# Gated delta attention and a GELU MLP on one core: the first chunk's inverse blocks go through DRAM on one queue, in the program's order

## The chip, the core and the metric

The kernel runs on one core of a Trainium2 chip. The core has five instruction streams that the profile names PE (TensorE, the matrix engine), DVE (VectorE), ACT (ScalarE), POOL (GpSimd) and SP (SyncE, which here only issues DMAs). DMAs are issued by SP, ACT and POOL. The metric is the device time of one execution in microseconds (us); lower is better.

## What is computed

Two blocks follow each other. The first is a delta-rule attention over 4 batches, 8 heads, 768 tokens and a head width of 48. The second is an MLP on the 3072 tokens with 384 inputs, 2048 hidden units and a sigmoid-approximated GELU. Cut to what matters:

```
k_n = k / (norm(k) + 1e-6)
for t in range(S):                      # per batch and head, state is 48 x 48
    y[t]  = q[t] @ state                # read before the update
    v_old = k_n[t] @ state
    state = state + beta[t] * outer(k_n[t], v[t] - v_old)
x = y, heads side by side               # 3072 x 384
h = x @ w_in                            # 384 x 2048, given as float64
out = (h / (1 + exp(-1.702 * h))) @ w_out   # 2048 x 384, given as float64
```

## The kernel before

**Chunks and units.** The 768 tokens are cut into 6 chunks of 128. A unit is one chunk of one batch (all 8 heads), so there are 24 units; units 0 to 3 are chunk 0, units 4 to 7 chunk 1. Within a chunk the recurrence is solved as a triangular system. The 128 tokens of a unit are four blocks of 32. For each head and block the inverse of a 32 x 32 triangular matrix is needed (tile `XB`, one per unit), and the rest is matmuls.

**What a unit needs.** `prepare(n)` transposes keys and queries on PE into `psT`, ACT copies them to `kqT` (L324), PE forms key-key and query-key products `psG` (L337), and ACT or DVE copies those into the SBUF tile `G` (L341, L343, L345). Then SP writes part of `G` to DRAM (`Nd`, L349) and reads its diagonal blocks back into `NT` with another layout (L355), and POOL masks the other half of `G` (L361).

**The inverse.** `invert(c, b0, nb)` takes the diagonal blocks in `NT`, one (batch, head, block) per partition, and inverts them on DVE by substitution: 15 steps of a multiply and a reduce (L401, L405 or, with the order kept, L104), then two rounds of four (L384, L385). For chunk 0 it runs once for all four batches on 128 partitions; for later chunks it runs for two batches at a time, mixed into the other work. Its result is scaled into `YS` (L435, tag `P`, which has two buffers that are also used by the temporaries of the weight conversion). `YS` has the wrong layout for PE, so each batch's quarter is written to DRAM (`Yd`, L439) and read back as `XB` (L444). In chunk 0, before the change, batches 0 and 2 use the SP queue and batches 1 and 3 the ACT queue. Each `XB` read waits for its `Yd` write.

**Solving.** Class `Step` holds a unit's chain: `solve` multiplies the inverse of a block with the values (`psU`, L490), `solved` copies to `U` on ACT (L497), `above` multiplies what has been solved into the next block (`psR`, L478), `rest` subtracts it from the values on DVE (`V`, L486). Four such rounds make a unit; `state` (L522, L530) and `outputs` (`psY`, L503; copies L542, L543; small DMAs L549 into `xT`) follow. `slot(n, share)` runs three units at different blocks side by side and puts pieces of the MLP between them.

**The MLP.** `hidden` multiplies `xT` with `w_in` (`ph`, L565) and applies the activation on ACT (`gT`, L570); `written` multiplies with `w_out` (`po`, L580), copies on DVE (L587) and stores. The weights come as float64 and are turned into float32 by bit operations in `from_double`: on DVE L167, then L173, L174, L175, L176, and for all but the first three pieces one step on ACT (L172) between L167 and L175. There are 12 pieces of `w_in` (the first three convert on DVE alone, pieces 4 to 12 with L172; they are called conversions 1 to 9 below) and 16 of `w_out`. POOL fetches most of the raw pieces (L239, L247) into space that earlier conversions have freed.

**Fillers.** `warm(n)` issues n matmuls on constants that only keep PE busy (`ps_warm`, L138): 80 at the start, 48 at the end of chunk 0's substitution, 6 in each of many groups of the first slots.

**Order.** The framework plans the order of instructions on each engine from its own estimates; the order in the program is only a starting point. An operation that goes through `pinned` (shown in profiles with line L104) keeps its place in the program's order. Each engine then works its list from front to back.

Of the kernel before, what the change touches and what calls it, by code (L numbers as in the profile page):

```python
# [18 lines left out]
def kernel(  # L19
# [19 lines left out]
    nc = tc.nc  # L39

    B, H, S, D = q.shape
# [60 lines left out]
    def pinned(op):  # L102

        return lambda *a, **kw: tc.keep_in_program_order(op(*a, **kw))  # L104
# [9 lines left out]
    for blk in range(NB):  # L114
# [10 lines left out]
        out=YB, in_=YB, compare_op=ALU.not_equal, fill=1.0, base=0,  # L125
# [6 lines left out]
    def warm(n, after=None):  # L132

        ps = ps_moe.tile([128, 256], F32, tag="moe", name="ps_warm")
        if after is not None:
            after(ps[:, 0:1], 0.0)
        for _ in range(n):
            nc.tensor.matmul(ps, lhsT=ones[:, 0:128], rhs=ones, start=True, stop=True)  # L138
# [229 lines left out]
    def invert(c, b0=0, nb=B):  # L368

        np = nb * NB * H  # L370
        part = slice(b0 * NB * H, b0 * NB * H + np)
        N, Y = NT[part], YB[part]
        bc = bI[part, c].broadcast_to([np, BS, BS])
        tt, red = nc.vector.tensor_tensor, nc.vector.tensor_reduce
        if c == 0:
            tt, red = pinned(tt), pinned(red)
        tt(N, N, bc, op=ALU.mult)  # L377
        yield 0.0
        HS = BS // 2

        def dots(o, a, b, ny, nx, nk, negate):

            P = wk.tile([128, ny, nx, nk], F32, tag="P", name="P")[part]
            tt(P, a, b, op=ALU.mult)  # L384
            red(o, P, axis=AX.X, op=ALU.add, negate=negate)  # L385

        def halves(t):

            return [t[:, s * HS : (s + 1) * HS, s * HS : (s + 1) * HS] for s in range(2)]


        Yf = Y.rearrange("p j i -> p (j i)")
        Nf = N.rearrange("p i k -> p (i k)")
        step = HS * BS + HS

        def diag(t, off, dims):
            return bass.AP(t.tensor, t.offset + off, [t.ap[0], [step, 2]] + dims)

        for i in range(1, HS):
            P = wk.tile([128, 2, i, i], F32, tag="P", name="P")[part]  # L400
            tt(  # L401
                P, diag(Nf, i * BS, [[0, i], [1, i]]), diag(Yf, 0, [[BS, i], [1, i]]),
                op=ALU.mult,
            )
            red(diag(Yf, i, [[BS, i]]), P, axis=AX.X, op=ALU.add, negate=True)  # L405
            yield 0.0


        X1 = N[:, 0:HS, HS:]
        nc.scalar.activation(X1, halves(Y)[1].rearrange("p l i -> p i l"), ACT.Copy)  # L410
        A = N[:, 0:HS, 0:HS]
        N10, Y0 = N[:, HS:, 0:HS], halves(Y)[0]
        Q = 4
        for j in range(0, HS, Q):
            n = HS - j
            dots(
                A[:, j : j + Q, :],
                N10[:, :, j:].rearrange("p (o l) k -> p o l k", o=1).broadcast_to([np, Q, HS, n]),
                Y0[:, j : j + Q, j:].rearrange("p j (o k) -> p j o k", o=1).broadcast_to([np, Q, HS, n]),
                Q, HS, n, False,  # L420
            )
            yield 0.0
        for i in range(0, HS, Q):
            n = i + Q
            dots(
                Y[:, 0:HS, HS + i : HS + i + Q],
                A[:, :, 0:n].rearrange("p j (o l) -> p j o l", o=1).broadcast_to([np, HS, Q, n]),
                X1[:, i : i + Q, 0:n].rearrange("p (o i) l -> p o i l", o=1).broadcast_to([np, HS, Q, n]),
                HS, Q, n, True,
            )  # L430
            yield 0.0
        if c == 0:
            warm(NY, pinned(nc.vector.memset))
        YS = wk.tile([128, BS, BS], F32, tag="P", name="YS")[part]
        nc.vector.tensor_tensor(YS, Y, bc, op=ALU.mult)  # L435
        for b in range(b0, b0 + nb):
            Yd = dram.tile([H * C, BS], F32, tag="Yd", name="Yd", bufs=4)
            eng = nc.scalar if c == 0 and b % 2 == 1 else nc.sync
            eng.dma_start(  # L439
                out=Yd.rearrange("(p j) i -> p j i", j=BS),  # L440
                in_=YS[(b - b0) * NB * H : (b - b0 + 1) * NB * H],
            )
            XB = wk.tile([128, H, BS], F32, tag="XB", name="XB", bufs=4)
            eng.dma_start(out=XB, in_=Yd.rearrange("(h t) i -> t h i", h=H))  # L444
            inverse[c * B + b] = XB
        yield 0.0


    def bank(name, shape=(128, H, D)):
        return ps_seq.tile(list(shape), F32, tag="seq", name=name)  # L450
# [3 lines left out]
    class Step:  # L454


        def __init__(self, n, xT):
            self.c, self.b = units[n]
            self.xT = xT
            self.kn, self.kqT, self.G = ready.pop(n)  # L460
            self.V, self.XB = loaded.pop(n), inverse.pop(n)
            self.psR = bank("psR")
# [25 lines left out]
        def solve(self, blk, h, psU):  # L488
            r = slice(blk * BS, (blk + 1) * BS)
            nc.tensor.matmul(  # L490
                psU[r, h, :], lhsT=self.XB[r, h, :], rhs=self.V[r, h, :],
                start=True, stop=True,
# [136 lines left out]
    def slot(n, share):  # L629
# [12 lines left out]
        for group in range(GR):  # L642
# [48 lines left out]
            if group == GR - 1 and n % HB == 1:  # L691

                m = n + 1 + HB
                if B <= m < len(units):
                    inverting = invert(*units[m], HB)
# [52 lines left out]
    for i in range(B, len(KN)):  # L748
        load(i, ((KN, k), (QP, q)), sync)
    ahead(2, sync)  # L750
    run(invert(0))
    normalize_first(B, len(KN) - B)
    run(weights(W1))
# [34 lines left out]
```

## Time and profile before

| what | value |
|---|---|
| median of 3 runs | 866.31 us (864.33 to 867.01) |
| profiled execution, its own time | 865.54 us |
| span of the profile | 863.8 us |
| PE busy | 813.2 us, 94% |
| PE weight loads busy | 601.8 us, 70% |
| DVE busy | 489.7 us, 57% |
| ACT busy | 208.6 us, 24% |
| POOL busy | 104.8 us, 12% |
| mean granted PE clock | 0.96 |

The span is the part of the execution that the profiler's records cover. All times in views of the profile count from its start. A line of a timeline gives the start, the length, the engine, the line of the kernel, the operation, the tiles as out<-in, the count, and in brackets how long the engine had been idle and what ended that.

### The profile page before, as it was taken

To read this page: it belongs to the slowest core of one execution; us is meant where nothing else is said; L and a number is where in the kernel's file an instruction comes from. 1 tells how busy PE (TensorE), PEld (TensorE's weight loads), DVE (VectorE), ACT (ScalarE), POOL (GpSimd) and SP (SyncE) were. 2 spreads that over 40 slices of the span, in tenths; PEclk is the share of its full clock that TensorE was granted. 3 is DMA by queue.
4 is the path that set the end of the run, shared out by engine and by line. 5 is a ranking of instruction groups with operands and counts; after the bars stand their busy time and mean duration, and the time that the engine had idled before them with its cause. 6 is when DMAs were issued, how large, how long until landed. Compare 5 with 4: busy or idle time off the path is not lost.

```text
span 863.8 us, 15545 instructions
## 1 busy us (share of the span) xinstructions
PE 813.2 (94%) x6564; PEld 601.8 (70%) x6564; DVE 489.7 (57%) x1024; ACT 208.6 (24%) x407; POOL 104.8 (12%) x117
## 2 busy tenths in 40 slices
PE   8309899989999999999999999999999999999998
PEld 7207688757767867867867767767767768677684
DVE  5898569979983592682682772772872851110100
ACT  3202345333212312312312312213212102112020
POOL 2103131230022102102102101101100000000000
PEclk9759759999999999999999999999999999999999
DMA  9995653451422223122132132132032020000000
GB/s 145 181 153 118 152 153 77 111 141 33 83 59 56 52 48 82 36 68 63 35 71 66 29 83 57 25 85 51 12 77 51 2 57 2 10 14 1 18 6 18
DMA packets 160964, 55.75 MB, mean 65 GB/s; under 512 B 128672, under 2 KB 157568, under 8 KB 160896
## 3 DMA queue, kind: packets, MB, share of 16 engines
q1 hardware_dynamic: 151872, 45.50, 26.0%
q0 software_dynamic: 1856, 7.87, 2.9%
q10 hardware_dynamic: 7168, 1.41, 1.3%
q8 instruction: 51, 0.84, 0.4%
q14 instruction: 17, 0.14, 0.1%
HBM read 33.13 MB, written 20.45 MB: 62 GB/s over the span
## 4 chain that ended last, share of the span: by engine, by line
PE 87%; DVE 7%; DMA 3%; issue 1%; ACT 1%; POOL 1%; ACTq 0%; DVEq 0%; POOLq 0%
PE ph L565 30%; PE po L580 28%; PE psG L337 6%; PE psR L478 5%; PE psY L503 5%; PE psU L490 4%; PE psR L467 2%; PE psT L323 2%; PE psS L522 2%; PE ps_warm L138 2%; DVE P L104 1%; DMA QP<-in_q_dram 1%; DVE YB L104 1%; DMA w_out<-in_moe_w_out_dram 1%; DVE tmp L104 1%
## 5 line engine op out<-in xcount | busy, mean ns | idle before, releaser
L565 PE MATMUL ph<-xT,w_in 128*128 128x256 f32 (+1 forms) x1248 | 270.1, 370 | 0.1
L580 PE MATMUL po<-w_out,gT 128*128 128x384 f32 x768 | 267.3, 493 | 2.2 <-DVE w_out L176 2.2
L565 PEld LDWEIGHTS ph<-xT,w_in 128*128 128x128 f32 x1248 | 219.8, 192 | 37.5 <-issue 9.6
L580 PEld LDWEIGHTS po<-w_out,gT 128*128 128x128 f32 x768 | 139.9, 190 | 92.4 <-issue 9.2
L486 DVE TENSOR_TENSOR V<-V,psR 32x384 f32<-32x384 f32 x92 | 50.6, 550 | 97.5 <-PE psR L478 91.7
L570 ACT ACTIVATE gT<-ph 128x512 f32<-128x512 f32 (+1 forms) x104 | 58.7, 564 | 186.9 <-PE ph L565 186.8
L497 ACT COPY U<-psU 32x384 f32<-32x384 f32 x96 | 45.1, 470 | 148.3 <-PE psU L490 99.5
L478 PEld LDWEIGHTS psR<-U,G 32*32 32x32 f32 (+2 forms) x1152 | 56.7, 112 | 23.7 <-issue 21.3
L138 PE MATMUL ps_warm<-ident 128*128 128x256 bf16 x260 | 35.8, 299 | 36.1 <-DVE ps_warm L104 33.0
L478 PE MATMUL psR<-U,G 32*32 32x48 f32 (+2 forms) x1152 | 67.3, 212 | 0.5 <-ACT U L497 0.5
L337 PE MATMUL psG<-kqT 48*128 48x256 f32 x384 | 62.2, 420 | 3.9 <-ACT kqT L324 2.8
L138 PEld LDWEIGHTS <-ident 128*128 128x128 bf16 x260 | 27.4, 107 | 43.1 <-DVE ps_warm L104 34.0
L490 PEld LDWEIGHTS psU<-V,XB 32*32 32x32 f32 x1536 | 39.6, 109 | 25.2 <-issue 12.2
L361 POOL TENSOR_SCALAR_AFFINE_SELECT G<-G 128x1024 f32<-128x1024 f32 x24 | 27.0, 1124 | 248.6 <-DVE G L345 112.1
L401 DVE TENSOR_TENSOR P<-NT,YB 64x2 f32<-64x2 f32 (+4 forms) x150 | 52.3, 349 | 4.6
L587 DVE COPY o<-po 128x384 f32<-128x384 f32 x24 | 13.3, 555 | 71.9 <-PE po L580 71.7
L405 DVE TENSOR_REDUCE YB<-P 64x2 f32<-64x2 f32 (+4 forms) x150 | 48.0, 320 | 4.4
L490 PE MATMUL psU<-V,XB 32*32 32x48 f32 x1536 | 47.6, 208 | 1.3 <-DVE V L486 1.3
L341 ACT ACTIVATE G<-psG 128x512 f32<-128x512 f32 x48 | 28.7, 597 | 76.4 <-PE psG L337 76.3
L337 PEld LDWEIGHTS psG<-kqT 48*128 48x128 f32 x384 | 37.4, 194 | 13.2 <-ACT kqT L324 4.0
L542 DVE COPY last<-psY 48x128 f32<-48x128 f32 x20 | 5.9, 294 | 59.1 <-ACT xT L543 58.2
L377 DVE TENSOR_TENSOR NT<-NT,bI 64x1024 f32<-64x1024 f32 x10 | 12.2, 1219 | 45.0 <-DMA NT<-Nd 44.9
(81 smaller groups left out, 713.7 us busy)
## 6 DMA issues: line engine op xcount, KB each, us to landing
Nd<-G SPq DMA_DIRECT2D x24, 512.0 KB, 3.2
w_out<-in_moe_w_out_dram POOLq DMA_DIRECT2D x14, 384.0 KB, 4.0
KN<-in_k_dram SPq DMA_DIRECT2D x24, 192.0 KB, 3.2
V<-in_v_dram SPq DMA_DIRECT2D x24, 192.0 KB, 3.3
out_dram<-o SPq DMA_DIRECT2D x24, 192.0 KB, 1.9
QP<-in_q_dram SPq DMA_DIRECT2D x20, 192.0 KB, 3.5
w_out<-in_moe_w_in_dram SPq DMA_DIRECT2D x6, 576.0 KB, 12.1
NT<-Nd SPq DMA_DIRECT2D x24, 128.0 KB, 2.5
```

The lines of the kernel that those rows point to most:

```text
L138: nc.tensor.matmul(ps, lhsT=ones[:, 0:128], rhs=ones, start=True, stop=True)
L337: nc.tensor.matmul(ps[hh][:, i], lhsT=kqT[pr, g + i, 0, :], rhs=kqT[pr, g + i, :, :], start=True, stop=True,)
L401: tt(P, diag(Nf, i * BS, [[0, i], [1, i]]), diag(Yf, 0, [[BS, i], [1, i]]), op=ALU.mult,)
L405: red(diag(Yf, i, [[BS, i]]), P, axis=AX.X, op=ALU.add, negate=True)
L478: nc.tensor.matmul(self.psR[r, h, :], lhsT=self.G[a, h, 0, r], rhs=self.U[a, h, :], start=(self.c == 0 and h == 0), stop=True, skip_group_ ...
L486: nc.vector.tensor_tensor(self.V[r], self.V[r], self.psR[r], op=ALU.subtract)
L490: nc.tensor.matmul(psU[r, h, :], lhsT=self.XB[r, h, :], rhs=self.V[r, h, :], start=True, stop=True,)
L497: nc.scalar.copy(self.U[r], psU[r])
L503: nc.tensor.matmul(self.psY[p : p + D, j, :], lhsT=lhsT(h), rhs=rhs(h), start=start and j == 0, stop=True, skip_group_check=True,)
L565: nc.tensor.matmul(ph[:, u], lhsT=w_in[:, j, f * 128 : (f + 1) * 128], rhs=xT[:, j, t], start=(j == 0), stop=(j == KC - 1),)
L570: nc.scalar.activation(gT[f0 // FQ][:, f0 % FQ : f0 % FQ + 2, t], ph, ACT.Gelu_apprx_sigmoid)
L580: nc.tensor.matmul(po, lhsT=gT[f // FQ][:, f % FQ, i * C : (i + 1) * C], rhs=w_out[:, f, :], start=(f == 0), stop=(f == FC - 1),)
```

## The change

For chunk 0 all four `Yd` writes and then all four `XB` reads are issued by SP, none by ACT, and they keep the program's order, which puts them directly behind the substitution. For the later chunks the queue was SP already; only the loop is split in two, so that both writes of a pair stand ahead of both reads in the program.

```diff
         YS = wk.tile([128, BS, BS], F32, tag="P", name="YS")[part]
         nc.vector.tensor_tensor(YS, Y, bc, op=ALU.mult)
+        dma = pinned(nc.sync.dma_start) if c == 0 else nc.sync.dma_start
+        back = []
         for b in range(b0, b0 + nb):
             Yd = dram.tile([H * C, BS], F32, tag="Yd", name="Yd", bufs=4)
-            eng = nc.scalar if c == 0 and b % 2 == 1 else nc.sync
-            eng.dma_start(
+            dma(
                 out=Yd.rearrange("(p j) i -> p j i", j=BS),
                 in_=YS[(b - b0) * NB * H : (b - b0 + 1) * NB * H],
             )
+            back.append(Yd)
+        for b, Yd in zip(range(b0, b0 + nb), back):
             XB = wk.tile([128, H, BS], F32, tag="XB", name="XB", bufs=4)
-            eng.dma_start(out=XB, in_=Yd.rearrange("(h t) i -> t h i", h=H))
+            dma(out=XB, in_=Yd.rearrange("(h t) i -> t h i", h=H))
             inverse[c * B + b] = XB
         yield 0.0
```

## The prediction

> **What bounds the kernel now.** I read the page first. Its second part cuts the span into 40 slices of 21.6 us.
>
> ```profile
> PE   8309899989999999999999999999999999999998
> PEclk9759759999999999999999999999999999999999
> DMA  9995653451422223122132132132032020000000
> ```
>
> From the tenth slice on (195 us) PE is busy and at full clock to the end. Whatever the change does before 195 us comes through only as a shift of the moment at which this dense part begins. So I read the chain that ended last, in order of time, around chunk 0's transfers:
>
> ```profile
> 86.83 1.19 PE psG L337 x8
> 88.05 4.02 DMA Yd<-YS
> 92.14 0.45 ACTq L444
> 92.69 0.60 ACTq L444
> 93.40 0.25 ACT tmp L172
> ...
> 94.73 0.98 ACT kqT L324 x2
> 95.75 0.79 PE psG L337 x2
> 96.54 1.41 PE psR L478 x16
> ```
>
> The reader is to see that the transfers on the ACT queue are on the path. Not because PE waits for `XB`: ACT stands at the `XB` issue until `Yd` has landed, and the copy `kqT` of unit 6 is queued behind. The timelines of ACT, PE and DVE show the three sides:
>
> ```profile
> 88.05 0.83 ACTq L439 DMA_DIRECT2D Yd<-YS  x2
> 88.97 0.72 ACT L172 ACTIVATE tmp<-tmp,low 128x512 int32<-128x512 int32 x1
> 90.38 0.59 ACT L343 ACTIVATE G<-psG 128x512 f32<-128x512 f32 x1
> 93.40 1.34 ACT L172 ACTIVATE tmp<-tmp,low 128x512 int32<-128x512 int32 x2 [2.42 <-DVE tmp L173]
> 95.59 0.45 ACT L497 COPY U<-psU 32x384 f32<-32x384 f32 x1
> ```
>
> ```profile
> 93.79 0.86 PE L490 MATMUL psU<-V,XB 32*32 32x48 f32 x16
> 95.75 0.79 PE L337 MATMUL psG<-kqT 48*128 48x256 f32 x2 [1.10 <-ACT kqT L324]
> 115.94 2.07 PE L337 MATMUL psG<-kqT 48*128 48x256 f32 x6 [0.59 <-ACT G L341]
> ```
>
> ```profile
> 89.73 0.69 DVE L175 SCALAR_TENSOR_TENSOR tmp<-w_out,tmp 128x512 int32<-128x512 int32 x1 [6.22 <-ACT tmp L172]
> 92.49 0.43 DVE L167 TENSOR_SCALAR tmp<-w_out 128x512 int32<-128x512 int32 x1 [1.34 <-DMA Yd<-YS]
> 122.03 0.56 DVE L486 TENSOR_TENSOR V<-V,psR 32x384 f32<-32x384 f32 x1 [1.59 <-PE psR L478]
> ```
>
> ACT lost 2.42 us; DVE lost 6.22 us for an L172 that ACT took late, and 1.34 us until `Yd` let go of `YS`, whose buffer conversion 5 needs. The first `psU` at 93.79 has no wait at all: what stands before it on PE are transposes and fillers. **Earlier `XB` tiles alone bring nothing.**
>
> **The clock** is the second thing to see.
>
> ```profile
> 94.00:96.00 2.00, 0.90 (x17) 0.77 (x15) 2.00 (x5) 2.00 (x5) 0.00 (x0) 1.00 1.22 253
> 96.00:98.00 2.00, 2.00 (x20) 1.46 (x19) 0.95 (x3) 0.04 (x1) 0.77 (x2) 0.56 0.95 150
> 120.00:122.00 2.00, 2.00 (x19) 1.38 (x17) 0.38 (x3) 0.60 (x1) 0.65 (x1) 0.50 0.83 143
> 126.00:128.00 2.00, 2.00 (x16) 2.00 (x16) 0.36 (x3) 0.77 (x2) 1.66 (x1) 0.76 0.26 47
> ```
>
> In this view of stretches the granted clock is the third number from the end. In quarter-microsecond stretches it falls at 96.2 and comes back at 126.9; earlier it changes at 24.6, 28.0, 34.8 and 68.9. All these moments lie a whole number of 3.41 us apart. Between 96.2 and 126.9 the small 32x32 matmuls keep PE busy and the clock stays at half; it returns only after a window of 3.41 us filled with `ph`. The window from 120.12 to 123.53, with 1.53 us of `ph` in it, did not suffice.
>
> **The change, part by part.** The order of instructions on each engine, of both kernels, says what moves; on ACT:
>
> ```
> before: G G Yd x2 tmp G G XB x2 tmp x2 kqT x2 U tmp U x2 tmp U x4 tmp last
> after:  G G G G tmp x2 kqT x2 tmp x2 U x3 tmp U tmp U x3 last
> ```
>
> (`G` is a copy, `tmp` an L172, `U` a copy of solved values.) On PE everything up to 93.79 is the same. Then before has `psU` x8 first and unit 6's `psG` x4 spread between the chain's steps; after has `psG` x4, then `psU` x8.
>
> **SP.** It issues two more `Yd` and four `XB` at 66 us, at 0.42 and 0.38 us each: 0.8 + 4 x 0.38 = 2.3 us. The slowest `Yd` landed 7.4 us behind its issue, so `XB` is issued from about 73.4 to 75 and landed (3.2 us the median, 7.4 us the slowest) by 83. SP's next instruction was `Nd` at 83.23. Cost nothing, covered by an idle SP from 66.8; without the cover `Nd` would be late, needed only by `NT` at 110.36 (L377). Later a `V` load stands ahead of one `NT` read. That load waited until 132.33, so `NT` goes from 124.5 to about 133; it is needed at 163.46. Nothing.
>
> **ACT, the gain.** The 2.42 us wait goes. But conversion 4's L172 now stands behind the four `G`. The last `G` starts at 90.38, so it starts at 90.38 + 0.49 = 90.87, against 88.97. Conversion 5 follows through DVE: L172 to L175 0.76 (88.97 to 89.73), L175 to L176 0.72, L176 to the next L167 0.73 (78.43 to 79.16), L167 to its L172 0.46 (79.16 to 79.62): 93.54. `kqT` 0.62 later at 94.16 (76.78 to 77.40), `psG` 1.13 after that (85.70 to 86.83): 95.29 against 95.75. **Of 2.42 us only 0.46 is left**; a chain through two conversions is late next. DVE's 1.34 us wait likewise turns into a later L167, 93.08 against 92.49.
>
> **PE and ACT, the loss.** `psG` x8 instructions 1.14 us at full clock, the last 0.21 doubled after 96.22: 96.64. `psU` x16 at half clock 1.41: the first `U` at 98.1, against 95.59, **2.5 us late**. (Two conversions stand before it on ACT: L167 of the second at 96.70, its L172 at 97.16, free at 97.78, just not the later of the two.)
>
> **PE, the way back.** The chain then runs without `psG` in it, each step by a row of before: `U` to `psR` 0.52 (105.25 to 105.77), `psR` to `V` 1.45 to 1.52, `V` to `psU` 0.61, `psU` to `U` 1.46, 1.52, 1.60. So `psR` 98.62, `V` 100.07, `psU` 100.68, `U` 102.14, `psR` 102.66, `V` 104.18, `psU` 104.79, `U` 106.31, `psR` 106.83, `V` 108.35, `psU` 108.97, `U` 110.57. Before that was 109.51: still 1.06 late. To the following `psR` the same work, 113.86 + 1.06 = 114.9; `V` 116.5; the next `psU` at 117.1, before at 117.94, because there three `psG` that waited for a copy stood in front. `U` 118.6, one `psG` 0.58 (four instructions took 1.16 at 97.95), `psR` 119.2, `V` 120.7 (122.03 before), three `psG` 1.72 to 122.4, `psU` x42 1.4 to 123.8, `ph` x8 2.0 and `psU` x4 0.15 to 125.95. Then 52 `ph` instructions: 4 at 0.25 us until 126.94, 48 at 0.118 us (30 took 3.54): 132.6. Before, the same work ended at 132.31. **PE is 0.3 us late.** DVE is 1.3 us early at its `V` with four small steps (0.7 us) still to do: 0.6 early.
>
> **The sum.** The chain runs through PE until 159.57, then ACT and DVE, where DVE had waited 0.55 us for ACT. So PE's +0.3 us decides. Against the profiled execution: 865.54 + 0.3 = 865.8; that run lies 0.8 below the median, which gives 866.6. I take 866.3, no change that can be measured. (A measurement of this kernel tells about 0.3%, 2.6 us, from no change.)
>
> The size I don't know is the clock. Before, 92.81 to 96.22 held transposes, `psU` and 0.5 us of `psG` and lost the clock; after, it holds 0.9 us of `psG` for the `psU`. The nearest row says it falls again; a window from 75.75 with 0.96 us idle kept it. If it holds until 99.63, `U` comes at 97.78 and `V` at 99.05, 1.0 us earlier: -0.7 in all. Such moments may also lie otherwise in each run. One window more or less at half clock over `ph` is 3.41 / 0.25 x (0.25 - 0.118) = 1.8 us either way.
>
> The Trainium skill, "TensorE: Matmul & The Clock Gate", Part 1, tells of a free-running window of 3413 ns, which the 3.41 us here agree with. It also lets the clock fall after an idle window; here it fell after one with 1.3 us idle of 3.41, so the measurement decides. By the page's rule the clock would not fall at 96.22 in the changed kernel, and the sum would be at or below the -0.7 just worked out.
>
> **Rivals.** *Faster:* the 2.42 us of ACT come out in full, since the conversions don't hold `kqT` up, and the clock holds one window longer: -2.4 - 1.0 = -3.4, 862.9. For it speak the 7.6 us that DVE waits there; against it the order on ACT, which puts two L172 before `kqT`. 22%.
> *Slower:* the first `U`, 2.5 us late behind `psG` and the conversions, isn't caught up, and `ph` then starts too late to bring the clock back at 126.94: 2.5 + 1.8 = +4.3, 870.6. It decides from `ph` starting after 126.94 - 1.53 = 125.4, 1.6 us later than my sum. For it speaks that the catching up rests on ten small gaps that I took from before; against it that in before `psG` filled only part of the gaps it stood in, and held a ready `psU` up at 115.94. 28%.
> *No change* (-0.7 to +0.8 around 866.3, and what lies within 0.3%): 50%. That the change doesn't do what it says is excluded by the order on SP.
>
> The range reaches to 863.0 and 870.2, leaving out about a tenth on each side. Faster by over 0.3% 0.22, within 0.50, slower 0.28.
>
> **What would show it.** After: no `Yd` or `XB` issue on ACT, all landed by 83; `kqT` of unit 6 at about 94.2; the first `psU` behind `psG` at 96.6, the first `U` at 98; `V` at 100; the fourth `U` near 110.6; `ph` from 123.8; clock back at 126.9. A first `U` before 96 or dense work from 192 would make me wrong on the fast side, a clock at half beyond 130 on the slow side.

## The result, and the profile after

| | median of the first runs | with the same kernel run again | profiled execution: its time, span, mean granted clock |
|---|---|---|---|
| before | 865.44 us (4 runs, 864.33 to 867.01) | 865.01 us (34 runs, 862.02 to 870.22) | 865.54 us, 863.8 us, 0.96 |
| after | 865.11 us (4 runs, 863.97 to 865.61) | 866.11 us (12 runs, 864.11 to 868.43) | 863.97 us, 862.2 us, 0.966 |
| ratio | 0.9993, 95% interval 0.9972 to 1.0014 | 1.0014, 95% interval 1.0000 to 1.0028 | |

No change that can be measured at the 0.3% named in the prediction. If there is one, it is a loss of about 1 us (866.11 against 865.01). In the views below the lines of the kernel after the change carry numbers 3 higher than in the kernel before, from the place of the change on (`psU` L493, `psR` L481, `U` L500); in e7 it is 4. Below, "first U" and "ph" are counted from the end of `YS` (the end of the substitution), because that moment itself lay between 65.0 and 68.0 us in the traces of this study, and does so for one and the same kernel (65.2, 68.0 and 67.4 us in three traces of after's instruction list). In the trace of before a window at half clock, from 24.55 to 27.96 us, lay on the first `psG` and in that of after none did; the end of `YS` is 0.8 us later there.

The slices of the page of after, PE's clock and PE first:

```profile
PE   8209799989999999999999999999999999999998
PEclk9759769999999999999999999999999999999999
```

PE's second and fifth slices and the clock's sixth differ by one tenth from before's; from the seventh on both lines read as before. The change is seen in the timelines around chunk 0's transfers. SP, ACT, PE and DVE of after:

```profile
65.17 1.72 SPq L104 DMA_DIRECT2D Yd<-YS  x4
69.39 2.60 SPq L104 DMA_DIRECT2D XB<-Yd  x4
```

```profile
89.58 0.59 ACT L343 ACTIVATE G<-psG 128x512 f32<-128x512 f32 x1
90.06 0.72 ACT L172 ACTIVATE tmp<-tmp,low 128x512 int32<-128x512 int32 x1
93.10 0.72 ACT L172 ACTIVATE tmp<-tmp,low 128x512 int32<-128x512 int32 x1 [2.32 <-DVE tmp L167]
93.72 1.06 ACT L324 ACTIVATE kqT<-psT 128x512 f32<-128x512 f32 x2
95.95 1.39 ACT L172 ACTIVATE tmp<-tmp,low 128x512 int32<-128x512 int32 x2 [1.16 <-DVE tmp L167]
97.25 0.45 ACT L500 COPY U<-psU 32x384 f32<-32x384 f32 x1
```

```profile
94.84 1.14 PE L337 MATMUL psG<-kqT 48*128 48x256 f32 x8 [1.78 <-ACT kqT L324]
95.91 0.86 PE L493 MATMUL psU<-V,XB 32*32 32x48 f32 x16
97.75 1.48 PE L481 MATMUL psR<-U,G 32*32 32x48 f32 x16 [0.98 <-ACT U L500]
```

```profile
90.81 1.07 DVE L175 SCALAR_TENSOR_TENSOR tmp<-w_out,tmp 128x512 int32<-128x512 int32 x1 [8.10 <-ACT tmp L172]
```

The wait at the `XB` issue is gone from ACT, and in its place stand 2.32 us in front of an L172: ACT waits for DVE's L167, and DVE had waited 8.10 us for the L172 before that one, which ACT took only after the last `G`. PE waits 1.78 us for `kqT`, which it did 1.10 us before, and now has the `psU` behind it. The first `U` on ACT starts at 97.25: its `psU` were done at 96.77, but two more L172 stood in front until then.

The chain of waits of after has the conversion on it, where before's had the transfer:

```profile
96.62 0.72 ACT tmp L172
97.34 0.37 ACT U L500
```

### The profile page after: what moved, and what is told of

Same layout as the page of the kernel before. It is cut to its first block, busy times and chain, and to the rows that moved or that the text cites. A ratio compares the mean times of both kernels' runs of the same rounds, so it can differ in the third digit from the quotient of the medians.

```text
span 862.2 us, 15547 instructions
## 1 busy us (share of the span) xinstructions
PE 806.3 (94%) x6564; PEld 597.2 (69%) x6564; DVE 490.7 (57%) x1024; ACT 208.7 (24%) x407; POOL 105.5 (12%) x117
## 4 chain that ended last, share of the span: by engine, by line
PE 83%; DVE 8%; DMA 5%; issue 1%; ACT 1%; ACTq 0%; POOL 0%; SPq 0%; DVEq 0%; POOLq 0%
PE ph L568 30%; PE po L583 28%; PE psR L481 5%; PE psY L506 5%; PE psG L337 5%; PE psU L493 4%; PE psR L470 2%; PE psS L525 2%; PE psT L323 2%; DMA w_out<-in_moe_w_out_dram 2%; DMA w_out<-in_moe_w_in_dram 1%; DVE P L104 1%; DMA bI<-in_beta_dram 1%; DVE YB L104 1%; DMA Nd<-G 1%
## 5 line engine op out<-in xcount | busy, mean ns | idle before, releaser
L500 ACT COPY U<-psU 32x384 f32<-32x384 f32 x96 | 45.0, 469 | 149.2 <-PE psU L493 99.4
L481 PEld LDWEIGHTS psR<-U,G 32*32 32x32 f32 (+2 forms) x1152 | 55.2, 110 | 23.9 <-issue 20.9
L138 PE MATMUL ps_warm<-ident 128*128 128x256 bf16 x260 | 33.9, 289 | 36.1 <-DVE ps_warm L104 33.0
L481 PE MATMUL psR<-U,G 32*32 32x48 f32 (+2 forms) x1152 | 65.7, 209 | 2.0 <-ACT U L500 2.0
L337 PE MATMUL psG<-kqT 48*128 48x256 f32 x384 | 58.4, 406 | 5.1 <-ACT kqT L324 4.0
L493 PEld LDWEIGHTS psU<-V,XB 32*32 32x32 f32 x1536 | 39.8, 110 | 27.7 <-issue 12.5
L361 POOL TENSOR_SCALAR_AFFINE_SELECT G<-G 128x1024 f32<-128x1024 f32 x24 | 26.7, 1111 | 249.8 <-DVE G L345 115.2
L401 DVE TENSOR_TENSOR P<-NT,YB 64x2 f32<-64x2 f32 (+4 forms) x150 | 51.9, 346 | 4.6
L590 DVE COPY o<-po 128x384 f32<-128x384 f32 x24 | 13.3, 555 | 71.8 <-PE po L583 71.7
L493 PE MATMUL psU<-V,XB 32*32 32x48 f32 x1536 | 48.0, 210 | 3.4 <-DVE V L489 3.4
L337 PEld LDWEIGHTS psG<-kqT 48*128 48x128 f32 x384 | 35.4, 188 | 14.3 <-ACT kqT L324 5.4
## 6 DMA issues: line engine op xcount, KB each, us to landing
w_out<-in_moe_w_in_dram SPq DMA_DIRECT2D x6, 576.0 KB, 11.7
```

The costliest lines, as they stand in the source:

```text
L337: nc.tensor.matmul(ps[hh][:, i], lhsT=kqT[pr, g + i, 0, :], rhs=kqT[pr, g + i, :, :], start=True, stop=True,)
L401: tt(P, diag(Nf, i * BS, [[0, i], [1, i]]), diag(Yf, 0, [[BS, i], [1, i]]), op=ALU.mult,)
L481: nc.tensor.matmul(self.psR[r, h, :], lhsT=self.G[a, h, 0, r], rhs=self.U[a, h, :], start=(self.c == 0 and h == 0), stop=True, skip_group_ ...
L493: nc.tensor.matmul(psU[r, h, :], lhsT=self.XB[r, h, :], rhs=self.V[r, h, :], start=True, stop=True,)
L500: nc.scalar.copy(self.U[r], psU[r])
```

## Experiments

**A ledger for all of them.** Each trace is cut at the end of `YS` and at the 481st `ph` (at 387 to 399 us), from which the span has 468.4 to 469.1 us left in every trace. Between these cuts PE works off the same 2769 matmuls in all kernels with six fillers a group, so that the stretches can be compared. The first `ph` is no such point: the planner puts 485 of them before it in the kernel before and 527 in the kernel after. In the stretch PE either is idle or is busy, and part of the stretch has the clock at half (read in steps of 0.05 us). All in us:

| kernel | end of YS | first U | first ph | PE idle | at half clock | stretch | span |
|---|---|---|---|---|---|---|---|
| before | 65.9 | +29.65 | +55.98 | 8.7 | 33.7 | 329.4 | 863.8 |
| e1, two queues in the program's order | 66.2 | +29.90 | +54.84 | 10.8 | 34.4 | 331.8 | 866.4 |
| after | 65.2 | +32.10 | +56.62 | 12.8 | 25.8 | 328.7 | 862.2 |
| e2, one queue, order free | 68.0 | +32.11 | +56.70 | 11.2 | 35.3 | 331.1 | 867.6 |
| e9, after again | 67.4 | +32.11 | +56.63 | 12.7 | 29.0 | 329.7 | 865.6 |
| e3, one queue, nine conversions on DVE | 65.9 | +29.70 | +50.61 | 11.9 | 31.2 | 330.9 | 865.4 |
| e4, two queues, the same | 67.3 | +26.73 | +49.65 | 13.3 | 29.1 | 331.6 | 867.3 |
| e5, one queue, no group fillers | 65.0 | +31.91 | +56.14 | 19.9 | 56.2 | 332.0 | 866.1 |
| e6, two queues, the same | 67.6 | +28.90 | +53.72 | 18.3 | 51.9 | 331.8 | 867.7 |
| e7, one queue, no sign for w_out | 65.2 | +32.11 | +56.62 | 13.1 | 29.2 | 330.0 | 863.6 |
| e8, two queues, the same | 65.1 | +29.56 | +53.48 | 9.4 | 25.7 | 326.8 | 860.3 |
| e10, one queue, two conversions on DVE | 65.0 | +30.68 | +53.87 | 11.7 | 29.4 | 328.9 | 862.3 |
| e11, two queues, the same | 66.8 | +29.60 | +53.73 | 13.6 | 27.0 | 329.8 | 865.0 |
| e12, one queue, ten fillers a group | 65.1 | +30.24 | +50.98 | 7.4 | 2.6 | 321.6 | 855.1 |

Over the eleven traces with six fillers a group, PE's busy time (stretch less idle) rises with the time at half clock by 0.48 us per us, by a straight line through them (standard error 0.08). So the stretch is, within 1.3 us, 303.8 + idle + 0.48 x half clock. The Trainium skill, "TensorE: Matmul & The Clock Gate", section "Terms", has a half-clock us cost half of itself; these traces agree. Two limits: around this line the six traces with one queue lie 1.1 us below the five with two, so it cannot settle differences of that size; and idle and half-clock time are not independent (from after to e2, with the same lists, half clock rises by 9.5 us and busy time by 4.0, but idle falls by 1.6). The stretches themselves are 329.9 us in the mean with one queue as with two.

### e1 and e2: is it the queue, or the order?

```diff
# e1: the kernel before, its transfers kept in the program's order
+by_queue = [nc.sync.dma_start] * 2 if c else [pinned(nc.sync.dma_start), pinned(nc.scalar.dma_start)]
...
-            eng = nc.scalar if c == 0 and b % 2 == 1 else nc.sync
-            eng.dma_start(
+            by_queue[b % 2](
# e2: the kernel after, order left to the planner
-        dma = pinned(nc.sync.dma_start) if c == 0 else nc.sync.dma_start
+        dma = nc.sync.dma_start
```

> The pin and the split loop alone: Yd and XB of chunk 0 keep the program's order, but batches 1 and 3 stay on the ACT queue. The list of instructions on every engine is that of the kernel before, so the pin does nothing here and the queue is the whole change. Theory (ACT's wait at the XB issue is what the queue removes): ACT waits again, 2.4 us ahead of conversion 5, DVE waits 1.3 us for Yd, first U about 1.8 us behind the last G copy's first psU as in before; time within 864.3 to 867.0. Rival (the pin is what matters): Yd on ACT issued near 66, no wait, and a trace like the changed kernel's. Second use: what differs between this trace and before's is chance from run to run; if the clock's windows and the 0.8 us by which the changed kernel's substitution ended early are chance, they move here too.

> The queue alone, without the pin: the list of instructions on every engine is that of the changed kernel. Theory: the trace of the changed kernel again, with conversion 4's L172 behind the four G copies, DVE idle about 8.1 us, first U about 7.7 us behind the start of the last G copy; time within 863.9 to 865.7 or so. Rival (the pin matters): Yd later than 66 and Nd ahead of it. Against the changed kernel only chance differs: I expect the window that held the full clock near 115 to 118 to be elsewhere or absent, worth about 1 us.

Measured, one run each: e1 868.15 us, e2 869.26 us, both longer than I had named; e2 has the window at full clock that I had expected to miss, at 116.9 us. The order of instructions of e1 is that of before on every engine; that of e2 is that of after. So keeping the program's order does nothing: **the queue alone is the change**. The first `U` comes at +29.7 and +29.9 with two queues, at +32.1 in all three traces with one. And the same lists of instructions gave spans of 863.8 and 866.4 us, and of 862.2, 867.6 and 865.6 us. That is more than the change is worth, and a single trace of each kernel cannot show its worth.

### e3 and e4: the conversions off ACT

```diff
         if alone:
...
+        elif n == 512:
+            ts(p, p, -896.0 * E1, 0.0, op0=ALU.add, op1=ALU.max)
+            ts(p, p, 255.0 * E1, 8.0, op0=ALU.min, op1=ALU.mult)
```

> The changed kernel, with the L172 step of the nine conversions of w_in done by two instructions on DVE instead of one on ACT (0.4 us each there). Theory (the chain through conversions 4 and 5 took the place of ACT's wait): DVE works through its 8.1 us of idle time, kqT of unit 6 starts when its transposes end, 1.2 us earlier against the last G copy, the first U 1.5 to 2 us earlier against it; of the time 1 to 2 us, ratio 0.997 to 0.999. Rival (that wait is not on the path, only the clock's windows set the time): first U earlier, but the dense part starts within 0.5 us of the changed kernel's, ratio 0.9995 to 1.0005. Rival (DVE is the bound in this stage): DVE's 7 us of extra work come out in the time, ratio 1.004 or more.

> The same edit in the kernel before. Theory: ACT still stands at the XB issue until Yd has landed, and DVE stands for YS until then, so of the idle time on DVE only the 6.2 us before conversion 4 are used; kqT comes by the two L172 ahead of it earlier, 1.3 us at most. Gain 0 to 1.3 us, less than in the changed kernel by about 1 us: ratio 0.9985 to 1.0005. Rival (the transfers' queue doesn't matter at all): the same gain as in the changed kernel, to within 0.3 us.

Measured: e3 868.91 us (ratio 1.0049, interval 1.0024 to 1.0075), e4 868.87 us (1.0055, 1.0032 to 1.0077). The gain that I expected of it did not come. Both are about 4 us slower than before and alike; the number is that of the rival by which DVE is the bound (1.004 or more). Yet `ph` starts 6.0 us earlier than in after (+50.61 against +56.62). That is order and not a lead: 90 small matmuls (58 `psU`, 32 `psR`) that stand before the first `ph` in after stand behind it in e3. The 438th matmul from the end of `YS` is that `ph` in e3, and after starts its own 438th at +51.18, only 0.6 us later. Over the whole stretch PE idles 0.9 us less in e3 than in after, but the clock is at half for 5.4 us longer, 2.6 us by the line above, and the stretch is 2.2 us longer. **An earlier `ph` is not an earlier end.** Whether DVE's added work or the clock makes the medians longer was not tried apart.

### e5 and e6: without the fillers in front of the first psU

```diff
-    NW, NA0, NY, NB0 = 80, 3, 48, 6
+    NW, NA0, NY, NB0 = 80, 3, 48, 0
```

> The kernel after, without the fillers that stand in groups in the first slots (the matmuls on constants that stand before the first psU in the kernel after and before). My theory (the start of the dense part is set by the conversion of w_out on DVE and its DMAs, not by PE's chain through chunk 0): the first psU may start earlier, ph with it by 1 to 3 us, but the first output copy moves by less than 1 us and the time stays within 0.4% of before: ratio 0.997 to 1.004, unless the clock loses more windows for want of fillers. Rival A (the early inverse blocks are worth something that the fillers hide): ratio 0.994 to 0.997, 2.5 to 5 us faster than before, and faster by over 2 us than the same kernel with two queues. Rival B (the fillers hold the clock up): half clock for four or more further windows before 130 us, ph later by 3 us or more; then ratio 1.004 or above if PE decides, and within 1.004 if the conversions decide.

> The kernel before (two queues), without the same fillers. My theory: within 0.4% of the kernel before, and within 2 us of the kernel with one queue and without fillers. Rival A: 2 us or more slower than that one, because the first psU here waits for ACT's queue. Rival B: as there, half clock for four or more further windows before 130 us.

Measured: e5 869.24 us (1.0046, 1.0032 to 1.0059), e6 868.89 us (1.0044, 1.0027 to 1.0062). Of Rival B the clock and the ratio came in both; a later `ph` did not (0.5 us earlier in e5, 2.3 in e6, with 107 fillers fewer in front). There is no difference between one queue and two. PE and ACT of e5:

```profile
90.97 1.48 PE L493 MATMUL psU<-V,XB 32*32 32x48 f32 x16
```

```profile
94.31 0.72 ACT L172 ACTIVATE tmp<-tmp,low 128x512 int32<-128x512 int32 x1 [2.13 <-DVE tmp L167]
96.31 0.72 ACT L172 ACTIVATE tmp<-tmp,low 128x512 int32<-128x512 int32 x1 [1.28 <-DVE tmp L167]
96.94 0.45 ACT L500 COPY U<-psU 32x384 f32<-32x384 f32 x1
```

Counted from the end of `YS`, the `psU` run 4.8 us earlier than in after (90.97 - 65.03 against 95.91 - 65.15), the `U` copy only 0.2: it stands behind four L172, of which the last three wait for DVE (the last two are shown). That shows the conversions as the late ones in the kernel with one queue and without fillers. Without fillers the clock is at half for 52 and 56 us instead of 26 to 35.

### e7 and e8: is the dense part waiting for w_out?

After e3 my theory was that the conversion of `w_out` sets when the dense part starts. The first output copy needs it, and the chain of waits of after runs from 146 to 191 us through DVE and the DMAs of `w_out`. e7 and e8 leave out one of DVE's steps there, the one that puts the signs back.

```diff
-        stt(out=p, in0=hi, scalar=-(1 << 31), in1=p, op0=AND, op1=OR)
+        if n == N_IN:
+            stt(out=p, in0=hi, scalar=-(1 << 31), in1=p, op0=AND, op1=OR)
```

> The kernel after, which leaves out the step of w_out's conversion that puts the sign back (L175, 0.47 us on DVE for each of 16 pieces, 7.5 us in all), so that w_out's signs are lost. My theory (the chain of w_out's conversions decides when the dense part starts): the first output copy comes 2 to 7.5 us earlier and the time falls by as much, ratio 0.991 to 0.998. Rival (PE's chain through chunk 0 to ph decides, as the prediction had it): the first output copy moves by less than 1 us, ratio 0.999 to 1.001.

> The kernel before (two queues) with the same step left out, so that w_out's signs are lost. My theory: the same gain as in the kernel with one queue, 2 to 7.5 us, ratio 0.991 to 0.998, and with the conversions relieved the two kernels' difference in PE's chain shows, if at all, with the 0.3 to 1 us by which the kernel with one queue is late there, less than can be measured. Rival: ratio 0.999 to 1.001.

Measured: e7 867.82 us (1.0034, 1.0020 to 1.0048), e8 867.99 us (1.0031, 1.0011 to 1.0050). Neither theory had that. The copies and PE, first of after, then of e7 (columns of the stretches: window, length, busy time of PE, PE loads, DVE, ACT, POOL, then clock, DMA share and GB/s):

```profile
199.68 0.56 DVE L590 COPY o<-po 128x384 f32<-128x384 f32 x1 [0.45 <-PE po L583]
```

```profile
180.00:200.00 20.00, 17.20 (x143) 10.12 (x142) 15.35 (x41) 6.60 (x14) 5.29 (x5) 1.00 0.37 88
```

```profile
191.10 0.56 DVE L591 COPY o<-po 128x384 f32<-128x384 f32 x1
202.02 0.56 DVE L591 COPY o<-po 128x384 f32<-128x384 f32 x1
```

```profile
140.00:160.00 20.00, 17.70 (x177) 15.67 (x176) 19.01 (x33) 7.95 (x18) 6.50 (x6) 1.00 0.57 120
180.00:200.00 20.00, 19.95 (x142) 11.64 (x139) 15.97 (x45) 5.90 (x13) 4.79 (x4) 1.00 0.33 83
```

The first copy comes 8.6 us earlier, the second 1.5 us later (in after it starts at 200.55), and the time is no shorter. The 2.8 us that PE idled from 180 to 200 us are gone, and 2.3 us stand from 140 to 160 instead (0.7 in after). **My theory falls**: PE is nearly full from `ph` on (after: 3.5 us idle from 122 to 394 us), so no chain that feeds it is worth more than those. Why both kernels are 0.3% slower with less to do on DVE stays open. What is left is the ledger: PE's work, its idle time, its half clock.

e7 and e8 also make the cleanest pair of single traces: `YS` ends within 0.05 us, and the clock falls at 97.7 in both. There the first `U` is 2.55 us later with one queue, `ph` 3.14, the 481st `ph` 3.25. But each trace is the fastest of its kernel's 12 runs; the medians are 0.2 us apart, the other way, and e8's own runs spread from 862.0 to 871.5 us.

### e9, e10 and e11: what makes the first U late

```diff
# e9: the kernel after, unchanged
# e10 in the kernel after, e11 in the kernel before:
-            from_double(dst, stages.pop(part), dst.shape[-1], part < NA)
+            from_double(dst, stages.pop(part), dst.shape[-1], part < NA, part in (6, 7))
...
-        if alone:
+        if alone or here:
             ts(p, p, -896.0 * E1, 0.0, op0=ALU.add, op1=ALU.max)
             ts(p, p, 255.0 * E1, 8.0, op0=ALU.min, op1=ALU.mult)
```

> The kernel after once more, for a narrower interval. Theory now (from the runs so far PE has hardly any idle time from 120 us on, so that the time is PE's work, plus PE's idle time, plus what half clock adds; the change makes PE idle 2 to 4 us longer between the substitution and ph, and how many windows at half clock follow differs from run to run by more): ratio 0.999 to 1.004, mean clock scattering by 0.01 and the times with it by about 5 us. Rival (the prediction's: PE is held up by 0.3 us only): ratio 0.999 to 1.001. Rival (the change is a gain that the first four runs hide): ratio below 0.998.

> The kernel after, with ACT's step (L172) of conversions 4 and 5 alone replaced by two steps on DVE, which stood idle there for 8 us; so no conversion stands on ACT between the last G and kqT of unit 6. Theory (the conversions in front of kqT are what makes the first psU late in the kernel after): kqT of unit 6 at 91.5 to 92.5 instead of 93.7, the first U 1.5 to 2.5 us earlier than in the kernel after (97.25), PE's idle time between the substitution and ph 2 to 3 us shorter, the time 1 to 4 us shorter: ratio to before 0.995 to 0.999. Rival (DVE's two added steps of each conversion come back as later conversions, as they did with all nine): ratio 1.001 or above. Rival (the first U is late for unit 6's psG, which stand before psU, and not for the conversions): first U within 1 us of the kernel after.

> The kernel before (two queues) with the same two conversions on DVE. Theory: here ACT's wait for Yd at its XB issue stays, and nothing is taken from in front of the first psU; the first U stays within 1 us of before's 95.59, the time within 0.3% of before. If the kernel with one queue and these conversions on DVE is the faster by 1 us or more, the queue change pays once its new wait is removed. Rival: both are slower than before by the same amount (DVE is what they wait for), ratio 1.001 to 1.005.

e9 is in the result above. PE's idle time between the substitution and `ph` is that of its first theory (9.4 us against 5.5 in before and 6.1 in e1); the ratio 1.0014, with an interval from 1.0000, fits that theory and leaves its rival (0.999 to 1.001) standing. e10 has 863.98 us (ratio 1.0002, 0.9982 to 1.0023), e11 866.70 us (1.0012, 0.9999 to 1.0024). By the medians e10 is 2.7 us better than e11, but by the ratios the two cannot be told apart, and the gain in time that e10's theory named (0.995 to 0.999) did not come; PE's idle time before `ph` is 0.9 us shorter than in after, not 2 to 3. ACT and PE of e10, then the same `kqT` in before:

```profile
92.61 1.08 ACT L324 ACTIVATE kqT<-psT 128x512 f32<-128x512 f32 x2 [2.55 <-PE psT L323]
95.71 0.47 ACT L500 COPY U<-psU 32x384 f32<-32x384 f32 x1 [0.80 <-PE psU L493]
```

```profile
93.75 1.14 PE L337 MATMUL psG<-kqT 48*128 48x256 f32 x8 [0.80 <-ACT kqT L324]
94.81 0.86 PE L493 MATMUL psU<-V,XB 32*32 32x48 f32 x16
```

```profile
94.64 1.06 ACT L324 ACTIVATE kqT<-psT 128x512 f32<-128x512 f32 x2
```

Now `kqT` waits for its transposes and the first `U` for its `psU`, no longer for a conversion. It comes at +30.68. So of the 2.45 us by which after is later than before (+32.10 against +29.65), 1.4 us are the conversions. The other 1.0 us come of the order: in e10 `psU` starts 1.9 us later than in before (94.81 - 65.03 against 93.79 - 65.94), because unit 6's eight `psG` (1.14 us) and a wait of 0.80 us for `kqT` stand in front of it; 0.9 us of this are won back, because in before the `U` stood behind `kqT` on ACT and here it does not. Both the theory and the rival that blamed the `psG` had a part of it.

### e12: more fillers

```diff
-    NW, NA0, NY, NB0 = 80, 3, 48, 6
+    NW, NA0, NY, NB0 = 80, 3, 48, 10
```

> The kernel after with 10 instead of 6 fillers in each group of the first slots (80 more matmuls on constants, at about 0.11 us at full clock 9 us of PE's time if they fill no gap). Theory (the time is PE's work, plus idle time, plus half clock): the fillers fill PE's idle time between the substitution and ph (9.3 us) and keep the clock up in one to three more windows (1.7 us each), but push the chain's matmuls back; together ratio 0.998 to 1.008, with the mean clock higher by 0.002 to 0.008. Rival (fillers are free, PE waits there anyway): ratio below 0.998. Rival (fillers only displace work): ratio 1.008 or above and the clock unchanged.

Measured: **859.67 us (11 runs, 856.79 to 864.66), ratio 0.9943, interval 0.9922 to 0.9964**: 5 to 6 us faster than both kernels. The number is that of the rival by which fillers are free; the reason is, by the ledger, the theory's, with a clock that gains more than I allowed (0.976 in the median of its runs against 0.961 in before's, where I had 0.002 to 0.008). Two stretches of 10 us, from 30 us after the end of `YS`, in after and in e12, and PE's timeline in e12:

```profile
95.15:105.15 10.00, 7.17 (x115) 6.10 (x113) 7.89 (x16) 3.31 (x6) 1.65 (x3) 0.63 0.38 123
105.15:115.15 10.00, 8.12 (x113) 7.01 (x110) 5.68 (x11) 3.24 (x8) 2.65 (x5) 0.52 0.44 117
```

```profile
95.06:105.06 10.00, 9.71 (x157) 7.77 (x155) 8.45 (x16) 4.04 (x8) 2.64 (x4) 1.00 0.86 238
105.06:115.06 10.00, 8.61 (x153) 6.25 (x152) 7.66 (x22) 5.67 (x13) 2.12 (x4) 1.00 0.59 185
```

```profile
94.88 1.16 PE L138 MATMUL ps_warm<-ident 128*128 128x256 bf16 x9
95.97 0.86 PE L481 MATMUL psR<-U,G 32*32 32x48 f32 x16
```

The second number from the left is PE's busy time, the third from the right the clock: it stays at full. In e12 fillers stand between the chain's steps, where PE waits for ACT and DVE anyway. The planner also moved unit 6's `kqT` behind, to 103.84 us, so that no `psG` stands before the first `psU`: first `U` at +30.24. The fillers and this move were not tried apart. By the ledger against e9: 5.2 us less idle (7.45 for 12.68) and 2.9 us less busy time (314.18 for 317.06), 8.1 us in all, though 80 fillers at 0.116 us (24 took 2.79 in before) add 9.3. This trace is the best of its 11 runs; the medians stand 6.4 us apart. Whether the kernel with two queues would gain as much was not tried.

## Why the prediction was right, step by step

The forecast, no change that can be measured, held: 866.3 was named, 865.11 and 866.11 were measured.

- **What is moved, SP.** As predicted: no issue on ACT, nothing late on SP. `XB` was issued from 69.39, 4.2 us behind the first `Yd` issue, not 73.4: the slowest landing was too dear an assumption. Nothing hung on it. `Nd` went 17.28 us behind the end of `YS` (at 82.43), in before 17.29.
- **"Earlier XB tiles alone bring nothing."** Held: the last `XB` is issued at 71.6 us and none took more than 3.4 us to land, and `psU` starts at 95.91, behind `psG`. In e5 `psU` came 4.8 us earlier and the `U` only 0.2.
- **ACT's gain, "of 2.42 us only 0.46 is left".** Right in kind, and even smaller: `kqT` of unit 6 is 0.13 us earlier (93.72 - 65.15 against 94.64 - 65.94). Conversion 4's L172 came where it was put (24.91 after `YS`, predicted 24.93); the next was 0.35 late, because L175 took 1.07 us where my row had 0.69.
- **The loss, "the first U 2.5 us late".** +32.10, predicted +32.16. But of the two that come together there I named the wrong one as the later: `psU` would end at half clock, I said, and the conversions be "just not the later of the two". The clock held until 97.7, `psU` ended at 96.77, and the L172 decided.
- **The way back.** 2.45 us at the first `U`, 1.3 at the fourth (110.03 - 65.15 against 109.51 - 65.94; I had 1.06), 0.6 at `ph`. The reason was the one given, that `psG` no longer stands in the chain: unit 6's eight `psG` took 1.14 us in one piece, before 0.79 + 1.23 + 1.22 = 3.24 us, most of it at half clock. `ph` at +56.62 was 1.2 us earlier than my +57.86, because one window in the middle (114.8 to 118.2) was at full clock. The traces e2 and e9 have such a window too, and so does e1 with two queues (114.2 to 117.6). It was not part of my sum. Two of the three `psG` pieces of before:

```profile
97.88 1.23 PE L337 MATMUL psG<-kqT 48*128 48x256 f32 x4
100.45 1.22 PE L337 MATMUL psG<-kqT 48*128 48x256 f32 x2
```

- **The sum, "the chain runs through PE until 159.57 [...] so PE's +0.3 us decides". This step was weak.** A lead or a lag of PE at one moment does not settle the end: after and e2, with the same lists, are 0.1 us apart at `ph` and 2.4 us apart at the 481st. What counts by the ledger is PE's idle time and its half clock. With one queue PE idles 11.2 to 12.8 us, with two 8.7 and 10.8: on the mean of three and two traces 2.5 us more. Half clock is 30.0 against 34.0 us, at 0.48 us each 1.9 us less. Together +0.6 us, out of two terms that I had not set against each other, and the second of which changes by as much from run to run. Nor do the traces show that +0.6: the stretches of the same five are 0.8 us shorter with one queue in the mean (329.8 against 330.6). So no run shows the +0.3, and that the forecast came this near is in part luck; what the runs show is that the effect is smaller than the scatter.
- **The clock.** I allowed 1.8 us for a window; 3.41 x 0.48 = 1.6 is what the ledger gives. That it moves by several windows from run to run was only hinted at ("may also lie otherwise in each run"), and it is the largest term of all: over 80 runs of the kernel before, the time falls by 4.5 us for each 0.01 of mean granted clock, between 0.954 and 0.968. (0.01 over the span is 17 us at half clock, which by the ledger would be 8 us; but half clock while PE idles, as from 33 to 64 us in after, costs nothing.) I also misread one window: the one that lost the clock at 96.22 had 1.10 us of idle time, not 1.3. In after the clock fell at 97.7, behind a window with 1.48 us of idle time of 3.41.
- **The rivals.** Faster: excluded by the interval of e9; its 2.42 us did not come out in full. Slower: the first `U` was late as it said, but was caught up; `ph` started at 121.77, before the 125.4 from which it was to decide. In e9 `ph` filled the window from 123.75 to 127.16 from 124.05 on, and the clock nonetheless came back only at 130.55, so the point from which it decides was not well founded.

**Open:** which matmuls in a window bring the clock back. After a window filled by `psS` and `psY` it rose at 114.8 in after (PE busy for all 3.41 us), and after a window much like it, from 109.9 to 113.3, it did not in before (3.26 us busy). And what the lag of PE is worth at the end: no pair of kernels here tells it from the scatter.

## What to carry to other kernels

Taking a wait off an engine brings only what the next thing in its queue allows. Here a 2.42 us wait for a DMA became 2.32 us for a conversion, and the reshuffled order made the chain's first step later. Where PE is full from some point on, don't follow one chain to its end: count PE's idle time and its time at half clock over a stretch with the same matmuls, since with the same matmuls only these can be won. In a stretch of small, dependent matmuls, filler matmuls in the gaps can be worth more than shorter gaps (here 5 us, together with a move of the planner's); and where runs of one kernel differ by its clock, one trace of each of two kernels does not tell them apart.

## What was not expected of the hardware

- The same instruction lists gave spans that differ by 2.6 us (before, e1) and by 5.4 us (after, e2), with the moments at which the clock changes falling elsewhere: first fall at 24.55 against 28.9 us, return at 125.0 against 130.6.
- A busy PE alone does not bring the clock back. In after PE was busy in the whole window from 118.2 to 121.6 us, with `psR`, `psG` and `psU`, and the clock stayed at half until 125.0; in e9 PE was busy from 120.3 to 130.6, over three windows, all at half clock. A stretch of after, then one of e9:

```profile
120.00:122.00 2.00, 2.00 (x45) 1.39 (x44) 1.80 (x8) 1.72 (x4) 0.66 (x1) 0.50 1.04 192
```

```profile
128.00:130.00 2.00, 2.00 (x12) 2.00 (x11) 1.07 (x7) 0.38 (x1) 1.40 (x2) 0.50 0.46 84
```

- Nor does PE's busy time alone say when the clock falls: a window with 2.31 us busy of 3.41 lost it in before (92.8 to 96.2), one with 2.16 us kept it in after (90.9 to 94.3).

- A DVE step took 1.07 us in after where the same form took 0.68 us in its neighbours (L175 at 90.81, against 79.77 and 94.04), with a POOL step (L361) running beside it. What slowed it was not tried.
